# A spectral filter and a feed-forward block on one core: other queues and another order in the first batch, and shrink's steps regrouped

## The chip, the cores and the metric

The kernel runs on one core of a Trainium2 chip. A core has five engines that each work through their own instructions in order: TensorE (PE in the profile, its weight loads PEld), VectorE (DVE), ScalarE (ACT), GpSimd (POOL) and SyncE (SP), which here only starts transfers. Transfers can also be started by ScalarE and by GpSimd. The metric is the time on the device in microseconds (us) from the first to the last instruction, the median of several executions.

## What is computed

Eight sequences of 3008 rows with 256 channels go through a Fourier transform along the rows, are multiplied with a complex filter and transformed back. Each row of the result then goes through a feed-forward block with 2048 hidden values and the activation h - tanh(h).

```python
def reference(x, filt_r, filt_i, w_in, w_out):   # x: (8, 3008, 256); cut to what matters
    X = np.fft.rfft(x, axis=1)
    Y = X * (filt_r + 1j * filt_i)[None]
    y = np.fft.irfft(Y, n=3008, axis=1).reshape(24064, 256)
    h = y @ w_in                                   # (24064, 2048)
    return ((h - np.tanh(h)) @ w_out).astype(np.float32)
```

The two weights arrive as 64-bit floats. [...]the kernel takes them as pairs of 32-bit words and assembles 32-bit floats with integer and float operations.

## The kernel before

3008 is split as 64 x 47. A first stage (`first`) transforms over 64 and writes to DRAM (`ct1`); a middle stage transforms over 47, multiplies with the filter, goes back over 47 and writes to DRAM (`ct2`); a last stage goes back over 64 and turns its result so that the feed-forward block can use it. The batches form five units: batch 0 alone, three pairs, batch 7 alone. While the feed-forward block works on one unit, the first and middle stages of the next are fed in between its matmuls, at the points called `t(0)` to `t(4)`. Only batch 0 has nothing to hide behind: its first and middle stage run before the main loop, and the weights are converted beside them.

The matmuls of the block use a scheme with seven products in place of eight, so a weight has seven blocks (`wu`, `wd`), of which GpSimd computes four from the others (`sums`). The conversion of one half of a quarter of the weights:

```python
def converted(tiles, src, dsts, queue, alone=False):
    t = tiles("raw", I64, n)
    queue.dma_start(t, src)                        # ... shortened
    yield
    V.tensor_scalar(out=it, in0=hi, ...)           # three operations on VectorE: L204, L205, L207
    V.tensor_scalar(out=pt, in0=hi, ...)
    V.tensor_scalar(out=st, in0=hi, ...)
    yield
    if alone:                                      # all on VectorE: L211, L213
        V.tensor_scalar(out=ft, in0=it, ...)
        V.tensor_scalar(out=pt, in0=pt, ...)
    else:                                          # or on ScalarE: L216, L217
        ACT.activation(ft, it, AF.Identity, bias=1.0, scale=2.0 ** -20)
        ACT.activation(pt, pt, AF.Relu, bias=exp_b)
    yield
    V.scalar_tensor_tensor(out=ft, in0=lo, ...)    # L219
    V.tensor_scalar_min(pt, pt, 255.0)             # L221
    yield
    V.scalar_tensor_tensor(out=pt, in0=pt, ...)    # L223
    for cols, dst, sign in dsts:
        V.scalar_tensor_tensor(out=dst, ...)       # L230
    yield
```

The first batch, cut to what the steps below need:

```python
xs = [load_x0(0, (0, 4, 8)), load_x0(1), load_x0(2)]      # halves on SP's and ScalarE's queue
ws = weights_alone(tiles0, range(3))                      # quarters 0 to 2, all on VectorE
...                                                       # memsets and the first filters, on GpSimd
mats = {0: load_slots(0, pro)}
next(ws)
for c in range(3):
    for k, _ in enumerate(first0(xs[c], c)):              # L883 matmul, L886 copy, L890 store
        if k == 3:
            next(ws)
G.dma_start(s2, s2_d)
turned(mats[0][1], gx[0])                                 # L915 copy, L916 times -1, on GpSimd
fts[1] = filters_of(1)                                    # six loads, L902
...
for _ in ws:
    pass
ws = weights(tiles0, range(3, 6), 2)                      # quarters 3 to 5, in rounds with ScalarE
next(ws)
...
for j in range(NK // 2):                                  # 16 steps of two slots each
    c = j // 2
    if j % 2 == 0 and c + 2 < NK // 4:
        a2[c + 2] = load_a2(0, c + 2, False, ("a2", "ft")[c % 2])
        mats[c + 2] = load_slots(c + 2, pro)
        fts[c + 2] = filters_of(c + 2)
    ...                                                   # two matmuls into pz (L996), back0() (L977 to L983)
    V.tensor_mul(uv, pz, ft[:, 0])                        # L1003
    V.tensor_mul(zs, pz, ft[:, 1])                        # L1004
    next(ws, None)
    if j % 2 and c + 1 < NK // 4:
        double_filters(fts[c + 1], c + 1)                 # two copies on ScalarE, L906, L907
        turned(mats[c + 1][1], gx[(c + 1) % 2])
    ...                                                   # near the end: first loads of the next unit, quarter 6
```

The main loop, one unit of it (192 in all). `d` and `e` are the steps of the second weight (`down`), `s` those of the activation (`shrink`), `t(k)` those of the other stages, of the stores and of the late conversion of quarter 7:

```python
def up(U, d, e, s, t):                                    # cut: setup of the banks X, Y, Z
    steps_at = ([1, 1, 1, 1, 0, 1, 1, 0] if U > 1 else [0, 0, 1, 0, 2, 0, 2, 1])
    mm(X, 1, True)
    mm(Y, 2, True)
    s1 = copied("s1")                                     # ScalarE, L551; u2 and u3 also
    t(0)
    d()
    shrinks(0)
    V.tensor_add(h[:, 0, :, 0:w], Y, s1)
    e()
    shrinks(1)
    t(1)
    mm(X, 6, False)
    mm(Z, 5, True)
    u2 = copied("u2")
    shrinks(2)
    d()
    shrinks(3)
    e()
    t(2)
    mm(X, 7, False)
    u3 = copied("u3")
    V.tensor_add(h[:, 3, :, 0:w], Z, u3)
    shrinks(4)
    d()
    shrinks(5)
    e()
    mm(X, 4, False)
    V.tensor_copy(h[:, 2, :, 0:w], X)                     # L589
    t(3)
    shrinks(6)
    d()
    e()
    t(4)
    mm(Z, 3, False)
    V.tensor_add(h[:, 1, :, 0:w], Z, u2)
    shrinks(7)
```

In the middle stage of the later units (L430 to L447) `pz` is read by two ScalarE operations (`zs`) and one multiply of VectorE (`uv`), and GpSimd does the rest; `pf`, `pz`, `pe` and `pu` of all stages share one PSUM bank in the main loop.

Of the kernel before, what the change touches and what calls it, by code (L numbers as in the profile page):

```python
# [143 lines left out]
def kernel(  # L144
# [117 lines left out]
        G.tensor_sub(w[:, 2], w[:, 1], w[:, 5])  # L262
        G.tensor_sub(w[:, 6], w[:, 0], w[:, 6])

    def begun(tiles, job, alone=False):
        j = converted(tiles, *job, nc.sync, alone)
        next(j)
        return j

    def weights(tiles, quarters, ahead):  # L270


        jobs = parts_of(quarters)
        began = [begun(tiles, job) for job in jobs[:ahead]]
        yield
        for k in range(len(jobs) + 1):
            if k < len(jobs):
                next(began[k])
            if k > 2 and k % 2:
                sums(quarters[k // 2 - 1])  # L280
            yield
            if k < len(jobs):
                next(began[k])
            if k > 0:
                for _ in began[k - 1]:
                    pass
            if k + ahead < len(jobs):
                began.append(begun(tiles, jobs[k + ahead]))
            yield
        sums(quarters[-1])  # L290
        yield

    def weights_alone(tiles, quarters):

        jobs = parts_of(quarters)
        began = [begun(tiles, job, True) for job in jobs[:2]]
        yield
        for k in range(len(jobs)):
            if k + 2 < len(jobs):
                began.append(begun(tiles, jobs[k + 2], True))  # L300
            for _ in began[k]:
                pass
            if k % 2:
                sums(quarters[k // 2])
            yield

    def weights_slow(tiles, quarters):

        jobs = parts_of(quarters)
        began = [begun(tiles, job, True) for job in jobs[:2]]  # L310
        yield
        for k in range(len(jobs)):
            for _ in began[k]:
                yield
            if k + 2 < len(jobs):
                began.append(begun(tiles, jobs[k + 2], True))
            if k % 2:
                sums(quarters[k // 2])
                yield
# [212 lines left out]
    def up(U, d, e, s, t):  # L532
# [21 lines left out]

        steps_at = ([1, 1, 1, 1, 0, 1, 1, 0] if U > 1 else [0, 0, 1, 0, 2, 0, 2, 1])

        def shrinks(at):
            for _ in range(steps_at[at]):  # L560
# [24 lines left out]
        d()  # L585
        shrinks(5)
        e()
        mm(X, 4, False)
        V.tensor_copy(h[:, 2, :, 0:w], X)  # L589
        t(3)  # L590
        shrinks(6)
        d()
        e()
# [5 lines left out]
    def shrink(U):  # L599

        h, w = hs.pop(U)
        ht = {k: h[:, k:k + 2].rearrange("p a b n -> p (a b) n")[:, :, 0:w] for k in (0, 2)}

        def tiles(tag, bufs):
            return dn.tile([128, 4, 256], F32, tag=tag, bufs=bufs, name=tag)[:, :, 0:w]

        y, sq = {}, {}

        def turn(k):
            y[k] = tiles("y", 2)  # L610
            ACT.activation(y[k], ht[k], AF.Arctan, scale=S)  # L611

        def power(k):
            ACT.activation(y[k], y[k], AF.Square,  # L614
                           accum_out=y_sums[:, 2 * U + k // 2:2 * U + k // 2 + 1])

        def times(k):
            V.tensor_mul(ht[k], ht[k], y[k])  # L618

        def square(k):  # L620
            sq[k] = tiles("sq", 1)
            ACT.activation(sq[k], y[k], AF.Square, bias=near_b, scale=A)  # L622

        def end(k):
            V.scalar_tensor_tensor(out=ht[k], in0=sq[k], scalar=K, in1=ht[k],  # L625
                                   op0=ALU.add, op1=ALU.mult)


        turn(2)
        power(2)  # L630
        yield
        times(2)
        yield
        square(2)
        turn(0)
        yield
        end(2)
        yield
        power(0)
        times(0)  # L640
        square(0)
        yield
        end(0)
        t = dn.tile([128, 4, 2, 256], F32, tag="t", bufs=2, name="t")
        blocks = [[h[:, 2 * a + k, :, 0:w] for k in range(2)] for a in range(2)]
        combine(blocks, [t[:, k, :, 0:w] for k in range(4)], U + 1 == 4 * len(groups))
        gs[U] = (blocks, t, w)
        yield
# [199 lines left out]
    with tc.tile_pool(name="tr", bufs=2) as tr, tc.manual_schedule():  # L848
        with tc.tile_pool(name="pro", bufs=1) as pro, \
# [6 lines left out]

            def big(shape, dtype, name):

                return pro.tile(shape, dtype, tag="big", bufs=3, name=name)

            def load_x0(c, cuts=(0, 8)):
                t = big([128, 8, DM], F32, "x0")
                for lo, hi in zip(cuts, cuts[1:]):
                    for h, rows, r, n in halves(0, 8 * c + lo, hi - lo):
                        (nc.sync, ACT)[h].dma_start(
                            t[rows, lo:lo + n, :],
                            dram(x.tensor, r * DM, [[NR * DM, 64], [1, n * DM]]))
                return t
# [26 lines left out]
            def filters_of(c):  # L895


                t = filt[c % 3]
                if c == NK // 4 - 1:
                    G.memset(t[IM:IM + 1, 1, 3], 0.0)  # L900
                for v, row, m, i, n, src in filter_rows(4 * c, 4 * c + 4):
                    G.dma_start(t[IM * v + row:IM * v + row + m, v, i:i + n], src)  # L902
                return t

            def double_filters(t, c):
                ACT.copy(t[IM:128, 0], t[0:IM, 0])  # L906
                ACT.copy(t[0:IM, 1], t[IM:128, 1])  # L907
                if c == NK // 4 - 1:
                    ACT.dma_start(t[IM:IM + 1, 0, 3, :],
                                  dram(filt_r.tensor, SEQ // 2 * DM, [[DM, 1], [1, DM]]))  # L910

            def turned(g3, t):


                G.tensor_copy(t[0:RP], g3[IM:IM + RP])  # L915
                G.tensor_scalar_mul(t[IM:IM + RP], g3[0:RP], -1.0)  # L916

            def tiles0(k, dtype, n):
                if k == "raw":
# [4 lines left out]
                return t if dtype == I32 else t.bitcast(dtype)  # L924

            conv = [None]
            filt = [pro.tile([128, 2, 4, DM], F32, name=f"filt{k}") for k in range(3)]
            nc.sync.dma_start(wf1, wf1_d)
            V.memset(near_b, B)
            V.memset(exp_b, -896.0)  # L930
# [1 line left out]

            ACT.activation(near_b, near_b, AF.Arctan)
            V.memset(near_b, B)
            ws = weights_alone(tiles0, range(3))

            pad = pro.tile([64, DM], F32, name="pad")
            G.memset(pad, 0.0)
            G.dma_start(dram(ct1[0], NR * 64 * DM, [[DM, 64], [1, DM]]), pad)

            for t in filt[0:1]:
                for v in range(2):
                    G.memset(t[IM * v + 32:IM * v + 64, v], 0.0)
            fts = {0: filters_of(0)}
            for t in filt[1:]:
                for v in range(2):
                    G.memset(t[IM * v + 32:IM * v + 64, v], 0.0)
            gx = [pro.tile([IM + RP, 4, RP2], F32, name=f"gx{k}") for k in range(2)]
            for t in gx:
                G.memset(t[32:64], 0.0)  # L950
            mats = {0: load_slots(0, pro)}
            next(ws)
            for c in range(3):
                for k, _ in enumerate(first0(xs[c], c)):
                    if k == 3:
                        next(ws)
            G.dma_start(s2, s2_d)
            turned(mats[0][1], gx[0])
            fts[1] = filters_of(1)
            a2 = {0: load_a2(0, 0, False)}  # L960
            mats[1] = load_slots(1, pro)
            a2[1] = load_a2(0, 1, False, "ft")
            double_filters(fts[0], 0)
            for _ in ws:
                pass
            ws = weights(tiles0, range(3, 6), 2)
            next(ws)
            e1s = pro.tile([128, 4, 2, DM], F32, name="e1s")
            waiting = []

            def back0():
# [14 lines left out]
            for j in range(NK // 2):  # L986
                c = j // 2
                if j % 2 == 0 and c + 1 < NK // 4:
                    if c + 2 < NK // 4:
                        a2[c + 2] = load_a2(0, c + 2, False, ("a2", "ft")[c % 2])  # L990
                        mats[c + 2] = load_slots(c + 2, pro)
                        fts[c + 2] = filters_of(c + 2)
                pz = z0("pz", [128, 2, DM])
                for i in range(2):
                    k = (2 * j + i) % 4
# [3 lines left out]
                    back0()  # L999
                uv = tr.tile([128, 2, DM], F32, tag="uv", bufs=2, name="uv")  # L1000
                zs = tr.tile([128, 2, DM], F32, tag="zs", bufs=2, name="zs")
                ft = fts[c][:, :, j % 2 * 2:j % 2 * 2 + 2]
                V.tensor_mul(uv, pz, ft[:, 0])  # L1003
                V.tensor_mul(zs, pz, ft[:, 1])  # L1004
                waiting.append((j, uv, zs))
                next(ws, None)
                if j % 2 and c + 1 < NK // 4:
                    double_filters(fts[c + 1], c + 1)
                    turned(mats[c + 1][1], gx[(c + 1) % 2])
                if j == NK // 2 - 3:  # L1010
                    fs = first(1, z1)
                    next(fs)
                    ws_gap = weights(tiles0, range(6, 7), 2)
                    next(ws_gap)
                if j == NK // 2 - 1:
                    e2s[0] = load_e2(*groups[0], None, slice(0, 48))
# [13 lines left out]
        with tc.tile_pool(name="dn", bufs=2) as dn, \  # L1030
# [32 lines left out]
                                     [[2 * NK * DM, m], [DM, n], [1, DM]]), src)  # L1063
                    yield

            late, copies = weights_slow(tiles1, range(7, 8)), filters_d()
            total = 4 * len(groups)
            for _ in last(0, z1):
                pass
# [121 lines left out]
```

## Time and profile before

| | |
|---|---|
| time, median of 3 | 2823.52 us (2822.45 to 2824.63) |
| span of the profiled execution | 2821.7 us |
| first matmul of the main loop (L545) | 123.83 us |
| chain that ended last, share of TensorE | 82% |
| moved by DMA | 217.53 MB, mean 77 GB/s |

The profile shows one execution. Busy time is the time in which an engine executed; a row of the timeline gives start and duration in us, engine and line (L12 is line 12 of the kernel before), operation, operands, how many instructions were merged, and in square brackets the idle time ahead of it with what ended it. A matmul on 32-bit floats appears as two records, so `x4` stands for two matmuls. A row of the stretches gives, after the stretch and its length, the busy time of each engine with its number of instructions, the clock granted to TensorE, the mean busy share of the 16 DMA engines and GB/s.

### The profile page before, as it was taken

Reading aid. Unit: us, or ns where it says so; the run is one execution under the profiler, and the core shown is the slowest. Engines: PE = TensorE matmul, PEld = TensorE weight load, DVE = VectorE, ACT = ScalarE, POOL = GpSimd, SP = SyncE. Lnnn points to the kernel's source line nnn. Section 1 sums busy time; section 2 is a strip of 40 time slices with the busy share of each in tenths; the row PEclk is TensorE's granted clock in tenths of the full one; section 3 lists DMA queues with packets and bytes.
Section 4 is the critical chain, followed back from the end, with each engine's and each line's share of the span. In section 5 each row is a group of like instructions: output and inputs, shape, how many; then the busy total and the mean of one; then the engine's idle time right before and its main releaser. Section 6 shows DMA issues by size and latency. Waiting matters only on the chain.

```text
span 2821.7 us, 36473 instructions
## 1 busy us (share of the span) xinstructions
PE 2727.4 (97%) x12438; PEld 2274.8 (81%) x12438; DVE 1915.9 (68%) x2175; ACT 1888.0 (67%) x2790; POOL 1769.1 (63%) x1407
## 2 busy tenths in 40 slices
PE   5899999999999999999999999999999999999998
PEld 2577777988878887888888888888888888898887
DVE  6755666656776777666676777666676676777776
ACT  2466676666767777666677777766666676666665
POOL 5546777544777767644586777654476666565654
PEclk7999999999999999999999999999999999999999
DMA  9854443233233322232333233112223222111010
GB/s 251 216 176 112 111 109 83 73 95 86 57 83 86 77 67 55 56 86 78 89 75 74 70 77 87 37 42 66 58 65 76 65 56 58 30 20 25 16 22 17
DMA packets 322591, 217.53 MB, mean 77 GB/s; under 512 B 224782, under 2 KB 274746, under 8 KB 322156
## 3 DMA queue, kind: packets, MB, share of 16 engines
q1 hardware_dynamic: 266826, 157.28, 24.0%
q10 hardware_dynamic: 52818, 51.53, 6.0%
q0 software_dynamic: 2752, 6.30, 0.8%
q8 instruction: 100, 1.64, 0.2%
q14 instruction: 95, 0.78, 0.1%
HBM read 138.87 MB, written 79.17 MB: 77 GB/s over the span
## 4 chain that ended last, share of the span: by engine, by line
PE 82%; DVE 6%; ACT 4%; POOL 2%; issue 2%; DMA 2%; ACTq 0%; DVEq 0%; SPq 0%; POOLq 0%
PE o L672 34%; PE x L545 21%; PE z L545 10%; PE y L545 5%; PE pe L411 3%; PE pz L430 3%; PE pu L511 3%; DVE h L618 2%; PE pf L351 2%; ACT y L614 1%; DVE h L589 1%; DMA raw<-in_moe_w_in_dram 1%; ACT y L611 1%; DMA filt<-in_filt_r_dram 1%; DVE uv L445 1%
## 5 line engine op out<-in xcount | busy, mean ns | idle before, releaser
L618 DVE TENSOR_TENSOR h<-h,y 128x1024 f32<-128x1024 f32 (+2 forms) x384 | 578.8, 1507 | 314.5 <-ACT y L614 313.1
L672 PE MATMUL o<-t,wd 128*128 128x256 f32 (+2 forms) x3072 | 777.0, 375 | 1.8 <-POOL t L526 1.3
L672 PEld LDWEIGHTS o<-t,wd 128*128 128x128 f32 x3072 | 580.9, 190 | 101.7 <-issue 30.4
L625 DVE SCALAR_TENSOR_TENSOR h<-sq,h 128x1024 f32<-128x1024 f32 (+2 forms) x384 | 559.0, 1456 | 117.7 <-ACT sq L622 109.7
L524 POOL TENSOR_TENSOR t<-h 128x512 f32<-128x512 f32 (+2 forms) x192 | 240.6, 1253 | 556.9 <-DVE h L625 398.2
L672 PE MATMUL o<-h,wd 128*128 128x256 f32 (+2 forms) x2304 | 584.0, 376 | 3.8 <-DVE h L625 3.8
L545 PE MATMUL x<-tu,wu 128*128 128x256 f32 (+2 forms) x2304 | 583.2, 375 | 4.4 <-ACT u L551 3.7
L545 PEld LDWEIGHTS x<-tu,wu 128*128 128x128 f32 x2304 | 430.8, 190 | 107.1 <-issue 45.0
L672 PEld LDWEIGHTS o<-h,wd 128*128 128x128 f32 x2304 | 431.6, 191 | 77.4 <-issue 16.5
L622 ACT ACTIVATE sq<-y,near_b 128x1024 f32<-128x1024 f32 (+2 forms) x384 | 435.2, 1133 | 6.5 <-DVE h L625 0.2
L611 ACT ACTIVATE y<-h 128x1024 f32<-128x1024 f32 (+2 forms) x384 | 397.4, 1035 | 14.4 <-ACT e L414 6.4
L614 ACT ACTIVATE y<-y 128x1024 f32<-128x1024 f32 (+2 forms) x384 | 399.9, 1041 | 6.5 <-ACT a L352 0.4
L551 ACT COPY s<-x 128x512 f32<-128x512 f32 (+2 forms) x192 | 110.9, 578 | 325.9 <-PE x L545 299.7
L527 POOL TENSOR_TENSOR t<-t,h 128x512 f32<-128x512 f32 (+2 forms) x192 | 319.1, 1662 | 0.1
L551 ACT COPY u<-x 128x512 f32<-128x512 f32 (+2 forms) x384 | 221.1, 576 | 141.6 <-PE x L545 129.2
L525 POOL TENSOR_TENSOR t<-h,t 128x512 f32<-128x512 f32 (+2 forms) x192 | 246.1, 1282 | 15.1
L526 POOL TENSOR_TENSOR t<-h 128x512 f32<-128x512 f32 (+2 forms) x191 | 245.7, 1287 | 0.0
L446 POOL TENSOR_TENSOR zs<-zs,ft 128x512 f32<-128x512 f32 x112 | 164.3, 1467 | 104.7 <-ACT zs L444 104.7
L447 POOL TENSOR_TENSOR uv<-uv,zs 128x512 f32<-128x512 f32 x112 | 207.4, 1852 | 9.1 <-DVE uv L445 0.5
L545 PE MATMUL x<-ut,wu 128*128 128x256 f32 (+2 forms) x768 | 198.0, 380 | 8.9 <-DVE h L589 7.8
L583 DVE TENSOR_TENSOR h<-z,u 128x512 f32<-128x512 f32 (+2 forms) x192 | 128.9, 671 | 113.3 <-ACT u L551 112.3
L545 PE MATMUL z<-tu,wu 128*128 128x256 f32 (+2 forms) x768 | 194.6, 376 | 0.0
(122 smaller groups left out, 3298.6 us busy)
## 6 DMA issues: line engine op xcount, KB each, us to landing
a<-ct SPq DMA_DIRECT2D x64, 384.0 KB, 4.0
ft<-filt SPq DMA_DIRECT2D x96, 256.0 KB, 4.7
out_dram<-ot SPq DMA_DIRECT2D x1392, 16.0 KB, 1.5
ct<-e ACTq DMA_DIRECT2D x112, 192.0 KB, 2.2
ct<-a ACTq DMA_DIRECT2D x80, 256.0 KB, 2.9
x_sb<-in_x_dram SPq DMA_DIRECT2D x69, 256.0 KB, 2.9
e<-ct SPq DMA_DIRECT2D x33, 512.0 KB, 4.3
fg<-fg SPq DMA_DIRECT2D x40, 392.0 KB, 5.8
```

The costliest lines, as they stand in the source:

```text
L524: G.tensor_sub(t[0], b[0][1], b[0][0])
L525: G.tensor_sub(t[1], b[1][1], t[0])
L526: (V if shared else G).tensor_sub(t[2], b[1][1], b[0][1])
L527: G.tensor_sub(t[3], t[1], b[1][0])
L545: nc.tensor.matmul(bank[:, k], wu[:, q - 1, (2 * u + k) * 128:(2 * u + k + 1) * 128], rhs[q - 1], start=(first and k == 0), stop=True, ski ...
L551: ACT.copy(t, X)
L611: ACT.activation(y[k], ht[k], AF.Arctan, scale=S)
L614: ACT.activation(y[k], y[k], AF.Square, accum_out=y_sums[:, 2 * U + k // 2:2 * U + k // 2 + 1])
L618: V.tensor_mul(ht[k], ht[k], y[k])
L622: ACT.activation(sq[k], y[k], AF.Square, bias=near_b, scale=A)
L625: V.scalar_tensor_tensor(out=ht[k], in0=sq[k], scalar=K, in1=ht[k], op0=ALU.add, op1=ALU.mult)
L672: nc.tensor.matmul(product(q), wd[:, q - 1, (2 * u + k) * 128: (2 * u + k + 1) * 128], rhs[q - 1][:, k], start=(u == 0 and k == 0 and q == ...
```

## The change

The first batch is arranged differently. x is loaded by SP's queue alone, but for one piece. The filters are loaded for eight slots at a time into two buffers in place of four slots into three. The raw weights of the first batch come by GpSimd's queue, and their conversions all go in rounds that share the work with ScalarE; quarters 0 to 4 run in these rounds, quarter 5 in the gap ahead of the main loop, and quarters 6 and 7 are converted inside the main loop, where before it was quarter 7 alone. The memsets of the filter buffers and of `gx` are VectorE's, and the multiplication by -1 in `turned` is ScalarE's. In the main loop the six steps of shrink are cut at other places, and t(3) stands ahead of the fourth matmul into X. The order of shrink in the kernel before was meant to keep ScalarE's long operations out of the way of the copies that TensorE waits for.

```diff
-    def begun(tiles, job, alone=False):
-        j = converted(tiles, *job, nc.sync, alone)
+    def begun(tiles, job, queue, alone=False):
+        j = converted(tiles, *job, queue, alone)
...
-    def weights_alone(tiles, quarters):
-        ...
@@ up
-        steps_at = ([1, 1, 1, 1, 0, 1, 1, 0] if U > 1 else [0, 0, 1, 0, 2, 0, 2, 1])
+        steps_at = ([1, 2, 0, 1, 0, 1, 1, 0] if U > 1 else [0, 0, 1, 0, 2, 0, 1, 2])
...
+        t(3)
         mm(X, 4, False)
         V.tensor_copy(h[:, 2, :, 0:w], X)
-        t(3)
@@ shrink
-        turn(2)
-        power(2)
-        yield
-        times(2)
+        start(2)                       # turn and power: ScalarE
         yield
-        square(2)
-        turn(0)
+        square(2)                      # times: VectorE, then square: ScalarE
         yield
         end(2)
         yield
-        power(0)
-        times(0)
+        start(0)
+        yield
         square(0)
         yield
         end(0)
@@ first batch
-                return pro.tile(shape, dtype, tag="big", bufs=3, name=name)
+                return pro.tile(shape, dtype, tag="big", bufs=2, name=name)
...
-                        (nc.sync, ACT)[h].dma_start(
+                        (ACT if h and c == lo == 0 else nc.sync).dma_start(
...
-                for v, row, m, i, n, src in filter_rows(4 * c, 4 * c + 4):
+                for v, row, m, i, n, src in filter_rows(8 * c, 8 * c + 8):
...
-                G.tensor_scalar_mul(t[IM:IM + RP], g3[0:RP], -1.0)
+                ACT.mul(t[IM:IM + RP], g3[0:RP], -1.0)
...
-            filt = [pro.tile([128, 2, 4, DM], F32, name=f"filt{k}") for k in range(3)]
+            filt = [pro.tile([128, 2, 8, DM], F32, name=f"filt{k}") for k in range(2)]
...
-            ws = weights_alone(tiles0, range(3))
+            ws = weights(tiles0, range(5))                 # raw weights by GpSimd's queue
...
-                    G.memset(t[IM * v + 32:IM * v + 64, v], 0.0)
+                    V.memset(t[IM * v + 32:IM * v + 64, v], 0.0)
...
-            for _ in ws:
-                pass
-            ws = weights(tiles0, range(3, 6), 2)
-            next(ws)
+            for _ in range(5):
+                next(ws)
...
-                        fts[c + 2] = filters_of(c + 2)
+                        if c % 2 == 0 and c > 0:
+                            filters_of(c // 2 + 1)
...
-                next(ws, None)
                 if j % 2 and c + 1 < NK // 4:
-                    double_filters(fts[c + 1], c + 1)
+                    double_filters(c + 1)
                     turned(mats[c + 1][1], gx[(c + 1) % 2])
+                next(ws)
...
-                    ws_gap = weights(tiles0, range(6, 7), 2)
+                    ws_gap = weights(tiles0, range(5, 6))
...
-            late, copies = weights_slow(tiles1, range(7, 8)), filters_d()
+            late, copies = weights_slow(tiles1, range(6, 8)), filters_d()
```

## The prediction

> **What bounds the kernel now.** I read the page's busy shares first, then the busy time in 20 us stretches, then the waits of TensorE, and last the timeline, once over the first batch and once over a unit of the steady loop.
>
> ```profile
> PE 2727.4 (97%) x12438; PEld 2274.8 (81%) x12438; DVE 1915.9 (68%) x2175; ACT 1888.0 (67%) x2790; POOL 1769.1 (63%) x1407
> ...
> core 0: us, PE busy (x) PEld busy (x) DVE busy (x) ACT busy (x) POOL busy (x), PEclk, DMA share, GB/s
> 0.00:20.00 20.00, 13.10 (x20) 4.75 (x20) 0.15 (x3) 3.83 (x6) 10.95 (x20) 1.00 0.94 239
> 20.00:40.00 20.00, 2.76 (x7) 0.96 (x6) 18.22 (x38) 6.53 (x11) 9.24 (x13) 0.63 0.89 281
> 40.00:60.00 20.00, 10.95 (x32) 7.54 (x32) 16.32 (x30) 3.27 (x5) 11.02 (x16) 0.60 1.02 262
> 60.00:80.00 20.00, 16.90 (x72) 11.88 (x72) 18.56 (x35) 12.86 (x19) 17.80 (x27) 1.00 0.90 218
> 80.00:100.00 20.00, 16.01 (x48) 10.76 (x48) 14.26 (x29) 8.68 (x12) 15.94 (x25) 0.74 1.05 266
> 100.00:120.00 20.00, 17.61 (x69) 12.58 (x68) 13.50 (x28) 9.50 (x15) 7.58 (x10) 0.91 0.62 177
> ```
>
> TensorE is busy for 2727.4 of 2821.7 us, so 94.3 us are idle. The six stretches sum to 77.3 busy of 120, so 42.7 of the 94.3 idle us lie in the first batch, before the loop over 192 units starts at 123.83. There the DMA share stays near 1 to 100 us, and VectorE and GpSimd are nearly full at 60 to 80. From 200 to 2822 TensorE is busy 2577.9 of 2622. The change cannot remove matmuls, so it can only move two things: the start of the loop, and some of the 44 us of gaps after 200.
>
> ```profile
> PE pe L411 <- DVE uv L445: 15.2, 16, 1.3
> PE pe L977 <- DVE uv L1003: 12.2, 7, 6.3
> PE pz L996 <- DMA a<-ct: 10.1, 1, 10.1
> PE x L545 <- DVE h L589: 7.8, 18, 0.9
> PE x L545 <- ACT u L551: 3.7, 4, 2.0
> ```
>
> The second and third rows are the first batch (columns: us in all, times, longest): 10.1 us for x to go through the first transform and back from DRAM, then 6.3 us for VectorE's first multiply.
>
> ```profile
> 51.04 0.76 DVE L230 SCALAR_TENSOR_TENSOR wu<-conv 128x256 f32<-128x256 f32 x2
> 51.72 0.68 DVE L1003 TENSOR_TENSOR uv<-pz,filt 128x512 f32<-128x512 f32 x1
> ...
> 91.93 0.69 DVE L1003 TENSOR_TENSOR uv<-pz,filt 128x512 f32<-128x512 f32 x1 [4.18 <-ACT filt L906]
> ```
>
> The first multiply follows at once on the sixth weight conversion: VectorE works one queue in order, and the six conversions of the form that needs no ScalarE fill it from 21.53 to 51.72. The data it needed was there near 43 (the first pz matmul starts at 42.44).
>
> ```profile
> 1510.42 0.59 ACT L551 COPY s<-x 128x512 f32<-128x512 f32 x1 [1.15 <-PE x L545]
> 1513.75 1.06 ACT L614 ACTIVATE y<-y 128x1024 f32<-128x1024 f32 x1
> 1516.13 0.59 ACT L551 COPY u<-x 128x512 f32<-128x512 f32 x1
> 1516.62 1.15 ACT L622 ACTIVATE sq<-y,near_b 128x1024 f32<-128x1024 f32 x1
> 1523.20 0.68 DVE L589 COPY h<-x 128x512 f32<-128x512 f32 x1
> ```
>
> This is one unit. The copies s1, u2, u3 (L551) and h2 (L589) read the bank X between accumulations, and TensorE's next matmul into X waits for each. Here u2 ends at 1516.72 and TensorE needs it at 1518.91; h2 ends at 1523.88 and is needed at 1524.96, 1.1 us later.
>
> **What the skill says.** "SBUF — State Buffer", Who interferes with whom: GpSimd and a VectorE instruction in a two-port mode hold a shared pair of ports exclusively, and a DMA from GpSimd's queue needs those ports for its descriptors. The trace agrees for compute: L205 takes 0.42 us alone and 0.95 at 30.14, inside GpSimd's sums. That descriptor writing starves is not seen: GpSimd's filter DMAs take 0.52 to 0.72 us beside the same VectorE work. The same page, Door 1: a transfer over 64 partitions reaches only half of the ports. Every load of x here covers 64; no run here times one alone. "DMA: Bandwidth & Descriptors", SWDGE vs HWDGE vs iDMA: each DMA engine goes round-robin between queues. The trace fits: to 37 us the SP queue moved 4.73 MB and the ACT queue 4.59.
>
> **The change part by part.** First, up to the first multiply. Before, 9.83 MB move to 37 us: x 3.08, its transform 3.08, five raw weights of 0.52, and the rest. After, three raws (two begun early, a third) but two filter batches of 0.77 MB in place of one of 0.39: 2.62 - 1.57 = 1.05 less and 1.15 more, the same bytes. x on one queue has one 64-partition load in flight at a time, so I let the x stage end 0 to 4 us later: pz at 42 to 46 instead of 42.44. On VectorE only job 0 and parts of jobs 1 and 2 stand ahead of the first multiply. Their last piece waits for ScalarE's conversion, behind the filter copies at 34 to 36: about 38 + 2.9 (L219 to L230) + 1.1 (L204 to L207) = 42. So the multiply starts at 43 to 46 against 51.72: **-6 to -9 us**.
>
> Second, the slot loop (16 steps). Before, 51.72 to 110.81 is 59.1 us: 32 multiplies of 0.60 (19.2), six conversions of 1.07 + 2.94 (24.1), and about 16 of waits and stretched instructions. After, eight second halves and seven first halves lie between the first and last multiply: 8 x 2.94 + 7 x 1.07 = 31.0, and 19.2, so 50.2. The waits: filter doubling (L906) now comes ahead of ScalarE's conversion of the round (1.3 us), GpSimd loses eight L916 of 1.2 us and 24 filter DMAs of 0.6, and ScalarE's stores share completion semaphores with fewer loads (89.22 minus the copy's end at 85.72 is such a wait). Against it: a raw load has 1.5 rounds of 6.8 = 10 us from issue to use and takes some 8 to land, and twice it stands behind a filter batch (6 x 0.6 = 3.6 us; 10 DMAs took 88.30 to 97.6). I leave 10 to 16 us of waits. The loop ends at 103 to 112 against 110.81. Together **-4 us** for the start of the main loop, give or take 7. The bytes bound this gain: by 100 us 25.3 MB have moved, and the change postpones only two raws, 1.05 MB, about 4 us at 262 GB/s.
>
> Third, those two raws: quarter 6 joins quarter 7 in the slow conversions inside the first units, two jobs of about 4.7 us on VectorE, now over 3.6 units instead of 1.8. In units 2 and 3 VectorE has 4 x 0.68 + 2 x 1.5 + 2 x 1.4 = 8.5 us of its own, plus five pieces of 1.2, against a period of 14. t(3) now stands ahead of the h2 copy, so a piece of 1.2 us delays TensorE. I take 2 us in each of units 2 and 3 and 1 before: **+5 us**.
>
> Fourth, the steady loop. Same instructions; the new order puts square(2) ahead of u2 and power(0) ahead of u3. From the end of the X matmul at 0: s1 to 0.6, turn, power, square 3.5 more, u2 done at 4.6 (6.2 where a 1.2 us zs pair and a p1 copy come in), needed at 6.0 (6.9 with the pz of that step). u3: 4.6 + 2.3 + 0.6 = 7.5, needed at 8.6. Slack of about 1 us remains, against 2 before: +3 us in the worst units. t(3) ahead of the h2 copy: if it holds pz, the chain pz, zs twice (1.44), uv, h2 ends 3.15 us after pz, and TensorE needs it at 3 x 0.86 = 2.58: 0.57 us in some 13 units, +7. Gains: t(3) to t(4) now has 1.73 us between them instead of 0.86, so the 1.34 us waits of L411 (five of them) fall to about 0.5, -4; and h2 comes earlier where t(3) is empty, because power(0) no longer follows u3, -3 of the 7.8. Sum **+3 us**.
>
> Total -4 + 5 + 3 = +4 us: 2823.5 + 4 = **2827.5**.
>
> **Rivals.** (a) The start moves much earlier: if VectorE's freed 9 us carry through and GpSimd's lighter load removes the 4.18 us and smaller waits, -12 us in the first batch, 2813 to 2816. For it: VectorE is the last wait at 51.72. Against: the DMA share near 1. (b) GpSimd's queue becomes the bound: raws, filters, sums and gx copies in one in-order queue, with eight completion semaphores in turn (a filter DMA at 73.95 waited 1.71 us on an earlier one). Each of six rounds losing 3 us makes +18, about 2845. (c) The old order of shrink costs every unit: 0.15 us in 192 units is 29 us, 2853. For it, u3's slack is 1.1 us and TENSOR_TENSOR stretches to 2.2 beside GpSimd; against it, VectorE's order hardly changes and ScalarE is 67% busy.
>
> **Range and chances.** The first batch carries +-10, the first units +-4, the steady loop -8 to +25, skewed up since slack shrinks. Range 2810 to 2852. 2% is 56 us, more than the 42.7 us idle in the first batch could give: faster by 2% has 0.01, slower by 2% 0.04, within 0.95.
>
> **What would show it.** The first uv multiply near 44 and no row of conversions ahead of it; the loop's first x matmul near 120 instead of 123.83; raw as a releaser of VectorE inside the slot loop if rival (b) is at work; TensorE idle between 140 and 200 up from 4.4 us by about 5; L545 waiting on L551 and on the h2 copy for under 20 us in all after 200. I am wrong if the loop starts after 130, or if those two waits exceed 30 us.

## The result, and the profile after

| | before | after |
|---|---|---|
| time, median of 6 | 2822.53 us (2819.88 to 2824.63) | 2831.46 us (2829.57 to 2833.41) |
| ratio, 95% interval | | 1.0033 (1.002 to 1.0046) |
| span of the profiled execution | 2821.7 us | 2830.5 us |
| first multiply uv of the first batch | 51.72 us | 50.27 us |
| first matmul of the main loop | 123.83 us | 126.30 us |
| chain that ended last, share of TensorE | 82% | 78% |
| TensorE idle from 140 to 200 us | 4.4 us | 3.9 us |

The change makes the kernel 0.33% slower, about 9 us. First the busy times on the page of the kernel after:

```profile
PE 2729.7 (96%) x12438; PEld 2267.0 (80%) x12438; DVE 1919.5 (68%) x2174; ACT 1887.4 (67%) x2806; POOL 1772.2 (63%) x1378
```

Then its first stretches of 20 us (the columns are those of the prediction's first fence):

```profile
0.00:20.00 20.00, 6.47 (x9) 2.36 (x10) 7.97 (x9) 3.83 (x6) 6.65 (x15) 0.90 0.94 186
20.00:40.00 20.00, 9.03 (x18) 3.42 (x16) 2.21 (x6) 5.22 (x11) 4.73 (x8) 0.76 1.03 265
40.00:60.00 20.00, 11.18 (x37) 8.16 (x38) 13.26 (x24) 9.91 (x15) 5.04 (x7) 0.66 0.92 225
60.00:80.00 20.00, 15.98 (x66) 10.20 (x64) 16.91 (x30) 11.41 (x17) 11.67 (x19) 1.00 1.05 266
80.00:100.00 20.00, 13.62 (x47) 9.21 (x46) 14.64 (x29) 12.26 (x17) 10.39 (x16) 0.83 0.90 247
100.00:120.00 20.00, 17.35 (x72) 11.70 (x70) 19.76 (x37) 11.59 (x18) 8.31 (x11) 1.00 0.68 192
```

TensorE is busy for 73.6 us of these 120, where it was 77.3. VectorE did lose its load: from 20 to 40 us it works 2.21 us instead of 18.22. But the DMA engines are as full as before, and x comes later: the first two stretches move 186 and 265 GB/s instead of 239 and 281. From 100 to 120 VectorE has hardly a gap left. TensorE's waits up to 124 us (us in all, times, longest):

```profile
PE pf L867 <- DMA x<-in_x_dram: 13.5, 3, 6.1
PE pe L957 <- DVE uv L985: 13.4, 11, 4.3
PE pz L977 <- DMA a<-ct: 10.6, 1, 10.6
```

and of the kernel before:

```profile
PE pf L883 <- DMA x<-in_x_dram: 6.9, 2, 5.7
```

The wait for x doubled; the wait for the transform to come back from DRAM (10.1 before) and the sum of the waits for the multiplies (12.2) changed little. Two rows of VectorE's timeline in the first batch:

```profile
50.27 0.69 DVE L985 TENSOR_TENSOR uv<-pz,filt 128x512 f32<-128x512 f32 x1 [4.04 <-PE pz L977]
...
82.86 0.43 DVE L204 TENSOR_SCALAR conv<-raw 128x512 int32<-128x512 int32 x1 [4.51 <-DMA raw<-in_moe_w_in_dram]
```

The first multiply no longer stands behind six conversions. It waits for TensorE instead, whose first pz matmul comes at 48.18 instead of 42.44. The way there, on ScalarE and TensorE:

```profile
30.61 1.07 ACT L870 COPY a<-pf 128x512 f32<-128x512 f32 x2 [7.11 <-DMA ct<-a]
...
36.48 1.11 PE L867 MATMUL pf<-x,wf_sb 64*64 64x256 f32 x2 [6.79 <-ACT a L870]
48.18 2.05 PE L977 MATMUL pz<-a,fg 94*128 94x256 f32 x4 [10.59 <-DMA a<-ct]
```

The copies out of the first stage stand for a store of that stage, the last pf matmuls for these copies, and pz for the load back. And later VectorE waits 4.51 us for a raw weight on GpSimd's queue.

Now the steady loop. TensorE's waits from 200 to 2760 us:

```profile
PE pe L398 <- DVE uv L432: 15.2, 23, 2.7
PE x L532 <- ACT u L538: 7.8, 23, 0.7
PE x L532 <- DVE h L577: 3.0, 7, 0.5
```

The first and last answer to 15.2 (16) and 7.8 (18) before; the middle one is new. The waits of the weight loads in the same window, of the kernel after:

```profile
PEld x L532 <- ACT u L538: 27.6, 62, 1.1
PEld x L532 <- DVE h L577: 19.9, 44, 0.9
```

and of the kernel before, in which weight loads hardly waited on u:

```profile
PEld x L545 <- ACT u L551: 1.3, 3, 0.4
PEld x L545 <- DVE h L589: 23.3, 39, 1.3
```

The start of a unit is the first matmul into bank Y. Comparing these starts, trace against trace, locates the loss. In this table a number is the start in that kernel less the start in the kernel before, in us; ratios are of times, with the 95% interval; "us" is the ratio less 1, times the time before of about 2821. A ratio compares all executions of a kernel with those of before taken beside them, and a start is that of one execution, so the two need not agree: the profiled execution of best was 4.3 us slower than its median, those of t3_first, square_early and shrink_only were 2.2, 3.9 and 5.0 us faster.

| kernel | ratio | us | unit 0 | 5 | 9 | 24 | 72 | 120 | 191 |
|---|---|---|---|---|---|---|---|---|---|
| after | 1.0033 (1.002 to 1.0046) | +9.3 | +3.30 | +2.20 | -1.72 | +2.16 | +7.27 | +12.43 | +11.92 |
| loop_only | 1.0043 (1.003 to 1.0056) | +12.1 | +0.24 | -2.20 | -4.43 | -0.51 | +4.82 | +10.63 | +10.21 |
| batch_only | 1.0003 (0.9995 to 1.0012) | +0.8 | +0.36 | +1.13 | +0.46 | +0.44 | +0.41 | +0.58 | +0.11 |
| t3_only | 1.0005 (0.9999 to 1.0012) | +1.4 | +1.38 | -0.34 | -1.02 | -4.77 | -2.00 | +0.77 | +0.86 |
| shrink_only | 1.008 (1.0067 to 1.0093) | +22.6 | -2.29 | -0.76 | -4.60 | +5.47 | +9.91 | +14.83 | +15.93 |
| power_early | 1.0043 (1.0029 to 1.0056) | +12.1 | -0.67 | +0.23 | -2.12 | -0.42 | +3.86 | +8.54 | +11.05 |
| square_early | 1.0021 (1.0014 to 1.0028) | +5.9 | -1.57 | -1.74 | -3.15 | -2.69 | -1.40 | -0.11 | +2.45 |
| batch_x_both | 0.9987 (0.9981 to 0.9994) | -3.7 | -1.70 | +0.79 | +0.04 | +0.03 | +0.04 | +0.20 | -0.21 |
| batch_raw_sp | 1.0005 (0.9997 to 1.0014) | +1.4 | +1.57 | +2.75 | +1.39 | +1.39 | +1.43 | +1.39 | +1.44 |
| batch_gap2 | 1.0054 (1.0041 to 1.0068) | +15.2 | +15.15 | +14.24 | +12.89 | +13.12 | +13.05 | +13.01 | +12.59 |
| t3_first | 0.998 (0.9971 to 0.9988) | -5.6 | -1.29 | -3.21 | -3.79 | -7.54 | -7.57 | -7.60 | -8.07 |
| best | 0.998 (0.9973 to 0.9987) | -5.6 | -1.30 | +0.99 | +0.66 | -3.04 | -3.04 | -2.88 | -3.21 |

How to read it: unit 0 is the first batch, and up to unit 5 the late conversions run. Units 0 to 23 are dense, each holding a large share of another stage; from 24 on the stages of a pair are spread over 48 units. In kernels with the first batch of before, unit 0 starts at 122.4 to 126.1, so +-2 us at unit 0 is within what one trace gives, and the +3.30 of after is not far beyond it. What happens inside the loop is steadier: after, loop_only and power_early all rise by 9 to 11 us from unit 24 to unit 120.

### The profile page after: what moved, and what is told of

It reads as the page before. It is cut to its first block, busy times and chain, and to the rows that moved or that the text cites. A ratio compares the mean times of both kernels' runs of the same rounds, so it can differ in the third digit from the quotient of the medians.

```text
span 2830.5 us, 36604 instructions
## 1 busy us (share of the span) xinstructions
PE 2729.7 (96%) x12438; PEld 2267.0 (80%) x12438; DVE 1919.5 (68%) x2174; ACT 1887.4 (67%) x2806; POOL 1772.2 (63%) x1378
## 3 DMA queue, kind: packets, MB, share of 16 engines
q0 software_dynamic: 3872, 12.59, 1.7%
## 4 chain that ended last, share of the span: by engine, by line
PE 78%; ACT 9%; issue 5%; DVE 4%; DMA 2%; ACTq 1%; POOL 0%; SPq 0%; DVEq 0%; POOLq 0%
PE o L650 32%; PE x L532 20%; PE z L532 9%; PE y L532 6%; PE pe L398 3%; PE pu L498 3%; PE pz L417 3%; ACT y L598 3%; PE pf L338 2%; ACT u L538 1%; ACT zs L431 1%; DVE h L604 1%; DVE uv L432 1%; ACT y L599 1%; ACT zs L430 1%
## 5 line engine op out<-in xcount | busy, mean ns | idle before, releaser
L604 DVE TENSOR_TENSOR h<-h,y 128x1024 f32<-128x1024 f32 (+2 forms) x384 | 571.1, 1487 | 270.4 <-ACT y L599 270.4
L608 DVE SCALAR_TENSOR_TENSOR h<-sq,h 128x1024 f32<-128x1024 f32 (+2 forms) x384 | 567.7, 1478 | 20.9 <-ACT y L598 0.5
L598 ACT ACTIVATE y<-h 128x1024 f32<-128x1024 f32 (+2 forms) x384 | 400.0, 1042 | 15.7 <-ACT e L401 8.1
L599 ACT ACTIVATE y<-y 128x1024 f32<-128x1024 f32 (+2 forms) x384 | 399.2, 1040 | 12.2
L514 POOL TENSOR_TENSOR t<-t,h 128x512 f32<-128x512 f32 (+2 forms) x192 | 309.0, 1609 | 0.1
L434 POOL TENSOR_TENSOR uv<-uv,zs 128x512 f32<-128x512 f32 x112 | 213.8, 1909 | 15.6 <-DVE uv L432 7.2
L556 DVE TENSOR_TENSOR h<-y,s 128x512 f32<-128x512 f32 (+2 forms) x192 | 130.3, 679 | 104.1 <-PE y L532 87.9
```

Of the source, the lines that this page charges most:

```text
L514: G.tensor_sub(t[3], t[1], b[1][0])
L599: ACT.activation(y[k], y[k], AF.Square, accum_out=y_sums[:, 2 * U + k // 2:2 * U + k // 2 + 1])
```

## The experiments

### Which half of the change it is

My theory after the two traces: the order of the loop costs the time, and the first batch little. loop_only is the kernel before with the loop of after; batch_only is the reverse, and so keeps the late conversion of two quarters.

```diff
# loop_only: before, and from the change only
-        steps_at = ([1, 1, 1, 1, 0, 1, 1, 0] if U > 1 else ...)
+        steps_at = ([1, 2, 0, 1, 0, 1, 1, 0] if U > 1 else ...)
+        t(3)
         mm(X, 4, False)
         V.tensor_copy(h[:, 2, :, 0:w], X)
-        t(3)
# and the steps of shrink as in the change
# batch_only: after, with steps_at, t(3) and the steps of shrink as before
```

Expected of loop_only:

> The first batch as before, the loop order as after. If the two halves of the change add up: first matmul of the loop at 123.8 as before, 20 to 25 waits on the copy u (L551) of some 8 us in all after 200, time +5 to +7 us (2828 to 2830). Rival, the loop order costs nothing by itself and the loss comes from the first batch: under 2 us.

Expected of batch_only:

> The first batch as after (with the late conversion of quarters 6 and 7), the loop order as before. If the halves add up: loop starts at 126 to 127, no wait on the copy u after 200, +2 to +4 us (2825 to 2827). Rival: +7 to +9, nearly all of the change.

Measured: 2832.47 and 2820.90 us beside 2820.97, ratios 1.0043 and 1.0003. loop_only costs about twice the 5 to 7 us expected, though its waits on u are as expected (8.0 us, 23 times); batch_only costs less than the 2 to 4 us expected. The loop is the whole loss, and the first batch is neutral as one piece.

### Which part of the loop's order it is

The loop's change has three parts: t(3) ahead of the fourth X matmul, and in the regrouped steps of shrink square(2) ahead of u2 and power(0) ahead of u3. With these, VectorE's end(2) also comes ahead of t(1) instead of behind u2; that was not run alone.

```diff
# t3_only: before, and
+        t(3)
         mm(X, 4, False)
         V.tensor_copy(h[:, 2, :, 0:w], X)
-        t(3)
# shrink_only: before with steps_at and shrink as in the change, t(3) not moved
# square_early: before, and in shrink
         times(2)
-        yield
         square(2)
+        yield
         turn(0)
# power_early: before, and in shrink
         square(2)
         turn(0)
+        power(0)
         yield
         ...
-        power(0)
         times(0)
         square(0)
```

Expected of t3_only:

> Before, with t(3) ahead of the fourth matmul into X and nothing else. Theory that t(3) is harmless: the 1.3 us waits of pe (L411) on uv fall to 0.5, the h2 waits stay under 10 us, time -2 to -5 us (2818 to 2821). Rival, that uv ahead of the h2 copy makes TensorE wait: 15 or more h2 waits of 0.5 us more, +4 to +8.

Expected of shrink_only:

> Before, with shrink's steps grouped as after and t(3) where it was. Theory that square ahead of u2 and power ahead of u3 are the loss: 20 or more waits on the copy u after 200 and +6 to +12 us (2829 to 2835). Rival, that ScalarE has slack enough: within 2 us of before.

Measured: t3_only 1.0005, no difference that can be measured, and so neither the theory's gain nor the rival's loss; shrink_only 1.008, +22.6 us, twice what was expected and much worse than the whole loop. The neutral sum of t3_only hides two opposite effects, which its waits from 200 to 2760 us show:

```profile
PE x L545 <- DVE h L590: 13.3, 39, 0.9
PE pe L411 <- DVE uv L445: 10.2, 16, 0.8
```

Before, these were 7.8 (18) and 15.2 (16). The waits on h2 gained 5.5 us and those of the inverse matmul on uv lost 5.0. The table shows where: t3_only gains 6.2 us by unit 24 (+1.38 to -4.77) and loses 5.6 after it (-4.77 to +0.86).

The two halves of the regrouping were then run alone. Expected of power_early:

> Before, with power(0) moved from after the copy u3 to just before it, nothing else. Theory that power ahead of u3 is what the regrouping costs (its rows before each wait end with power, then the zs pair of t(2), then u3): 20 or more waits of u3, +15 to +22 us as the regrouping alone, 2836 to 2843. Rival, that square ahead of u2 is the loss: under 4 us.

Expected of square_early:

> Before, with square(2) moved from after the copy u2 to before it, nothing else. Theory: u2 has the slack of 1 us, no waits of u2, within 3 us of before. Rival: +10 us or more.

Measured: power_early 1.0043, +12.1 us, somewhat under its theory; square_early 1.0021, +5.9 us, between its theory and the rival: TensorE waited for u2 only 4 times after 200 us, but its weight loads 30 times. The two together are 18.0 of shrink_only's 22.6 us. What is left was not run alone. In the traces it lies ahead of unit 24, where shrink_only loses 7.8 us, power_early 0.3 and square_early nothing. The waits of power_early from 200 to 2760 us:

```profile
PE x L545 <- ACT u L551: 9.3, 22, 1.3
PE x L545 <- DVE h L589: 4.0, 14, 0.5
```

That is the new row of the kernel after, from one moved operation, and the fall of the h2 row that goes with it: with power(0) out of the way, fewer h2 copies are late. The trace of after shows the mechanism in a unit whose t(2) holds a slot. ScalarE and TensorE, timeline of after:

```profile
805.16 1.06 ACT L598 ACTIVATE y<-h 128x1024 f32<-128x1024 f32 x1
...
806.25 1.06 ACT L599 ACTIVATE y<-y 128x1024 f32<-128x1024 f32 x1
...
807.42 0.59 ACT L430 ACTIVATE zs<-pz 64x512 f32<-64x512 f32 x1
808.03 0.58 ACT L431 COPY zs<-pz 64x512 f32<-64x512 f32 x1
808.63 0.59 ACT L538 COPY u<-x 128x512 f32<-128x512 f32 x1
...
809.27 0.73 PEld L532 LDWEIGHTS x<-tu,wu 128*128 128x128 f32 x4 [0.74 <-ACT u L538]
809.27 1.13 PE L532 MATMUL x<-tu,wu 128*128 128x256 f32 x4 [0.33 <-ACT u L538]
```

The same unit of before:

```profile
803.65 0.58 ACT L444 COPY zs<-pz 64x512 f32<-64x512 f32 x1
804.25 0.59 ACT L551 COPY u<-x 128x512 f32<-128x512 f32 x1
804.73 1.06 ACT L614 ACTIVATE y<-y 128x1024 f32<-128x1024 f32 x1
...
805.16 0.84 PEld L545 LDWEIGHTS x<-tu,wu 128*128 128x128 f32 x4
805.38 1.03 PE L545 MATMUL x<-tu,wu 128*128 128x256 f32 x4
```

ScalarE works in order. Before, it does turn(0), the two zs, u3, and then power(0) (L614). After, it does turn(0) (L598), power(0) (L599), the two zs of t(2), and then u3. The copy ends at 809.22 and TensorE, done with the matmul ahead at 808.94, stands. Before, u3 ends at 804.84, half a microsecond before it is needed, and the weights are loaded 0.22 us ahead of their matmul. After, weights and matmul start together, and the four records take 1.13 us instead of 1.03.

The last point explains why TensorE's own wait rows show too little. From the start of unit 24 to that of unit 191 both traces hold the same 10503 TensorE records, at a full clock in both, and after takes 9.8 us longer. Only 1.5 us of that is idle time; the same records last 8.2 us longer. (The ends of matmul records are modelled, so this split is the profile's; the 9.8 us are between starts.) Worked out from the records of the two traces:

| after less before, unit 24 to 191, us | idle ahead | longer records |
|---|---|---|
| matmuls into X behind u2 | +1.5 | +3.1 |
| matmuls into X behind u3 | +6.0 | +5.8 |
| first matmuls into X, behind h2 | -4.2 | -0.1 |
| all others | -1.8 | -0.5 |

The same count for power_early gives +17.7 us behind u3, nothing behind u2 and -5.7 behind h2; for square_early +4.9 behind u2 and nothing behind u3. So each move costs where the copy behind it stands, and nowhere else by more than 2 us.

### What bounds the first batch

Three variants of batch_only. batch_x_both puts x back on both queues. batch_raw_sp puts the raw weights back on SP's queue. batch_gap2 moves quarter 6 from the first units into the gap ahead of the main loop.

```diff
# batch_x_both: batch_only, and
-                        (ACT if h and c == lo == 0 else nc.sync).dma_start(
+                        (nc.sync, ACT)[h].dma_start(
# batch_raw_sp: batch_only, and
-            began = [begun(tiles, job, G) for job in jobs[:2]]
+            began = [begun(tiles, job, nc.sync) for job in jobs[:2]]
-                    began.append(begun(tiles, jobs[k + 2], G))
+                    began.append(begun(tiles, jobs[k + 2], nc.sync))
# batch_gap2: batch_only, and
-                    ws_gap = weights(tiles0, range(5, 6))
+                    ws_gap = weights(tiles0, range(5, 7))
-            late, copies = weights_slow(tiles1, range(6, 8)), filters_d()
+            late, copies = weights_slow(tiles1, range(7, 8)), filters_d()
```

Expected of batch_x_both:

> The first batch as after but x on both queues, the loop order as before. Theory that x on one queue delays the transform: first pz at 42 to 45 instead of 48, and the loop starts where VectorE's chain allows, 2 to 5 us earlier, time -2 to -5 us against the batch alone. Rival, that the bytes set the pace: pz moves under 2 us and the time under 2 us.

Measured: 0.9987. The first pz matmul comes at 44.57 instead of 49.11, the first multiply at 46.65 instead of 51.19, and the loop's first matmul at 121.29 instead of 123.35. Up to 37 us 9.38 MB have moved instead of 8.32. "SBUF — State Buffer" of the Trainium skill says under "Can I just issue two DMAs to hit both halves?" that two concurrent transfers, one on each half of the partitions, measured only 6% over one, because they serialize. Here, with x on two queues, all queues together moved 13% more in the same 37 us, at the same busy share of the DMA engines (0.97 and 0.98). The page speaks of two transfers and no others beside them; for this kernel the measurement decides: x on one queue holds the first batch back. The start's gain of 2.1 us over batch_only is mostly gone by unit 5 (+0.79 against +1.13), and at unit 191 the two traces differ by 0.3 us, though their ratios differ by 0.0016, 4.5 us. The two were not timed side by side; how much of this reaches the end stays open.

Expected of batch_raw_sp:

> The first batch of the kernel after with the raw weights on SP's queue as before; the loop of before. Theory that GpSimd's queue holds the raw weights back: the 4.5 us and 1.2 us for which VectorE waits for raw in the slot loop fall under 1 us in all, the last multiply comes 2 to 5 us earlier, time 2817 to 2819. Rival, that the bytes set it: the waits for raw stay or turn into waits for a2 or for the filters on ScalarE, x is later by the raw weights that now share its queue, and the time is 2820 to 2824.

Measured: 1.0005, as batch_only. VectorE's waits for raw do not vanish: 5.43 us just ahead of the first multiply, then 1.29 and 3.37. The first pz matmul comes earlier, not later (46.39, in batch_only 49.11), but the first multiply is at 52.04 (51.19 in batch_only) and the last at 110.14 (107.59). Moving the raw weights only moves who waits. GpSimd's queue is not the bound; this speaks for the bytes, without measuring them alone.

Expected of batch_gap2:

> The first batch of the kernel after with quarter 6 converted in the gap, not in the first units; the loop of before. Theory that the loop starts when VectorE ends the last conversion of the gap: two more halves of about 4 us move the first ut copy and the first matmul of the loop from 123.4 to 128 to 132 us; time 2824 to 2829 (+3 to +8 against the 2820.9 of the same kernel with quarter 6 in the first units). Rival, that the loop starts when the loads and matmuls ahead of it are through (the last multiply plus 13 us): the start stays at 122 to 125, and the time within 2 us of 2821. If a late half costs what the prediction said (2.5 us each of the +5), the first units also give 2 to 3 us back.

Measured: 1.0054, 15 us, more than either theory had. VectorE and ScalarE at the end of its gap, timelines of the two engines:

```profile
134.87 0.83 DVE L230 SCALAR_TENSOR_TENSOR wd<-conv 128x256 f32<-128x256 f32 x3
...
135.93 0.58 ACT L500 COPY ut<-pu 128x512 f32<-128x512 f32 x1 [6.46 <-DVE wd L230]
```

The first ut copy, from which the loop's first matmul follows, starts 0.23 us after the last conversion of the gap ends (135.70). So it does in all 13 traces, 0.23 us in each: before 121.97 and 122.20, after 123.96 and 124.19, best 118.96 and 119.19. The loads and matmuls ahead of it are no bound: in batch_gap2 the first pu matmul is at 117.63, and the ut copy 18 us later. The theory is confirmed, and its size was too small, in large part because the second round of the gap waited 4.77 us for its raw weight. The rows of before and after name a raw load as the releaser of that copy; those of batch_gap2 and batch_only name VectorE. Why it waits is an inference: ut is allocated where the first batch's buffers lay.

It also gives a bound for the late conversion. Against batch_only, batch_gap2 starts the loop 14.8 us later and its unit 191 12.5 us later, so quarter 6 in the first units costs at most 2.3 us. It may be less: batch_gap2 gains as much on before (+15.15 to +12.89 by unit 9), which has the same one late quarter, so the gain may come from the later start.

### A version that beats both kernels

t(3) early pays in the dense units and costs in the others. t3_first is the kernel before with it early only in the first 24 units; best is batch_x_both with the same.

```diff
+        if groups[i][0] == 0:
+            t(3)
         mm(X, 4, False)
         V.tensor_copy(h[:, 2, :, 0:w], X)
-        t(3)
+        if groups[i][0] > 0:
+            t(3)
```

Expected of t3_first:

> Before, with t(3) ahead of the fourth matmul into X only while the first batch runs in the loop (24 units), where stages follow each other at every t. Theory that t(3) ahead gains in the dense part what it loses in the pairs: it keeps the 5 us gained by unit 24 and has h2 waits as before, -4 to -6 us (2815 to 2817 where before is 2821). Rival: the gain is noise of the first batch, within 2 us.

Expected of best:

> The first batch of the kernel after with x on both queues, and the loop of before with t(3) ahead of the fourth X matmul in the first 24 units alone. If the two gains seen apart add up (7.8 us of 2822 for t(3), 3.7 us for the first batch), the time is 2811 us, ratio 0.996; the start of the loop stays near 121 us and the gain by the end of the first 24 units is about 7 us. If both gains are the same idle time (the first units run into the late conversions, which t(3) placed earlier brings ahead of the h2 copy), it is 2814 to 2818, no better than t(3) alone.

Measured: t3_first 2814.73 beside 2821.16, ratio 0.998 (0.9971 to 0.9988); best 2816.08 beside 2821.6, ratio 0.998 (0.9973 to 0.9987). Both beat both kernels, by 0.2% of before. The waits of t3_first from 200 to 2760 us keep the better half of t3_only and not the worse:

```profile
PE pe L411 <- DVE uv L445: 11.6, 16, 1.2
PE x L545 <- DVE h L591: 7.8, 18, 0.9
```

The gains don't seem to add up: the sum would be 0.9967, a little outside the interval of best, and both terms are uncertain themselves. In the traces best gains 3.7 us from unit 9 to 24, as t3_first does (3.75), but from unit 0 to 5 it loses 2.3 where t3_first gains 1.9. batch_x_both loses 2.5 there too, with t(3) in its old place, so it isn't t(3) that brings the late conversion ahead of the h2 copy, as the second expectation had it; it is the late quarter itself, or what else the first units share with it (batch_only, with the same late quarter, loses 0.8); this stays open. The new first batch brings nothing measurable beside t3_first.

## Why the prediction was right or wrong

The time was predicted as 2827.5 us, 4 above before, in a range of 2810 to 2852. It came to 2831.46, 9 above. The range and the direction held, but none of the three terms of its sum (-4 for the start, +5 for the late conversions, +3 for the steady loop) came out as stated.

**First multiply, -6 to -9 us: wrong.** It came 1.5 us earlier, at 50.27. VectorE was free, as the step said (2.21 us of work from 20 to 40). The term that failed is "pz at 42 to 46 instead of 42.44": it came at 48.18. "I let the x stage end 0 to 4 us later" was too short, and it was 5.3 (the last pf matmuls start at 36.48 instead of 31.19). The loads of x on one queue did land one after another (in batch_only the first three are issued at 1.18, 1.86 and 2.49 and land at 5.72, 8.11 and 10.45). But the step counted only them, and the end of the stage hangs on its stores: the first store took from 10.16 to 28.87 to land, before from 10.13 to 20.41. batch_x_both gets pz back to 44.57 though its x stage ends no sooner (last pf matmuls at 34.81, in batch_only 34.94): the load back from DRAM is issued at 40.31 instead of 42.83, and pz follows 4.3 us later instead of 6.3.

**Slot loop, 50.2 + 10 to 16 us of waits: right.** From the first multiply to the end of the last it took 61.9 us (50.27 to 112.13), 11.7 more than 50.2. The two waits on raw for which the margin stood are there, 1.23 and 4.51 us. So rival (b) was at work, but batch_raw_sp shows that it was not GpSimd's queue that made it.

**Together -4 us for the start: wrong**, by the first step. The loop began at 126.30 instead of near 120. Of the 2.5 us above before, 1.3 are the later end of the last multiply and 0.7 the conversions behind it. Most of it is within what one trace of the same code varies by (121.5 to 125.2 with the first batch of before), and batch_only puts the whole first batch at +0.03% (-0.05 to +0.12). What the step did not see is that the loop's start hangs on the end of the conversions in the gap and not on the slot loop's data. There one more half conversion now stands behind the last multiply (112.13 to 114.65); it costs little, since VectorE waited 3.9 us for ScalarE in the gap of before.

**Late conversions, +5 us: too large.** TensorE's idle time from 140 to 200 us went from 4.4 to 3.9 instead of up by 5. The fair comparison is loop_only, with the same loop and one late quarter: from unit 0 to 5 it gains 2.44 us and after gains 1.10, so the second late quarter cost 1.3 us, and by unit 9 the difference is gone; batch_gap2 gives at most 2.3.

**Steady loop, +3 us: the right mechanism with one size wrong.** From unit 24 to 191 it cost 9.8 us. The failed piece is "u3: 4.6 + 2.3 + 0.6 = 7.5, needed at 8.6. Slack of about 1 us remains". The 2.3 are turn(0) and power(0); what other steps put between power(0) and u3, in order on ScalarE, was left out. With t(2)'s two zs operations (1.2 us) u3 is at 8.7, and the slack is gone. I had counted the zs pair for u2 and not for u3. It is not the only such operation: of the 6.1 us that TensorE stood for u3 from unit 24 on, 3.1 fall to 8 units with the zs pair, 2.3 to 8 units with the copy of pe in its place and 0.7 to 5 units with the copy p5. The loss of both u copies was priced at +3 us; in after it is 16.4 (11.8 behind u3, 4.6 behind u2), of which earlier h2 copies give 4.3 back. Moving power(0) alone measures +12.1 (8.2 to 15.8), and square(2) ahead of u2, which the step also named, +5.9.

The other pieces were closer. For "0.57 us in some 13 units, +7", t(3) ahead of h2, the wait row of t3_only gives +5.5, and +11.0 with the longer records from unit 24 to 191. The gain of 4 on the waits of L411 was 5.0. "h2 comes earlier", -3 of the 7.8, was -3.8 in power_early (7.8 to 4.0). What the sum did not see is that these pieces are not independent: with the regrouped steps early t(3) costs nothing from unit 24 on (loop_only +10.7, shrink_only +10.5) and gains 8.5 us in the dense units, so loop_only has +12.1 where shrink_only has +22.6.

**How near the sum came is in part luck.** In the trace of after the start is +3.3 us (predicted -4), units 0 to 5 give -1.1 (+5), units 5 to 24 nothing and the rest +9.8 (+3): the errors of the first two terms nearly cancel.

**Rivals.** (a), a much earlier start, needed the 9 us that VectorE was freed by, and the later pz took most of them. (c) was the right kind, a small cost in many units; of the 29 us that it gave, loop_only measured 12.

**The test that was too weak.** I said that I would be wrong if the waits of L545's line on u and h2 exceeded 30 us. They were 10.8 after 200 us, and still the loop lost some 12. The rows of the weight loads (47.5 us against 24.6) would have pointed to the place, but they do not rank the losses: shrink_only, which lost most, has 42.7, and t3_only, which lost nothing in all, has 37.0 on h2 alone.

## What to carry to other kernels

When a step is moved on an in-order engine, list everything that stands between the bank's last matmul and the copy that frees the bank, other stages' operations included, and compare it with the time to the next matmul. Do so for every kind of unit, with each operation that can stand there; an average load of 67% says nothing of it. Read the waits of the weight loads beside those of the matmuls, and compare the starts of like units in two traces: a late weight shows as a longer busy matmul. A move that is neutral as a whole may be two effects of opposite sign in two phases of the kernel, and then it is worth making in one phase only.

## What was not expected of the hardware

- A matmul that waits for a bank begins together with its weight load, and its records stretch: four took 1.13 us instead of 1.03, beside the 0.33 us of idle time shown. From unit 24 to 191 this hid 8.2 of 9.8 us in busy time.
- With the two halves of x on two queues, all queues together moved 9.38 MB by 37 us, with nearly all of x on one 8.32, at the same busy share of the DMA engines, and the first pz matmul came 4.5 us earlier.
- The copy that starts the main loop named a raw load as its releaser in the traces before and after, but started 0.23 us behind VectorE's last conversion in all 13 traces. Lengthening VectorE's work by one quarter moved it by 15 us.
